# A fused attention and expert kernel: the second head's leftover keys moved to its front, and second scores of two row blocks formed on GpSimd

## The chip, the cores and the metric

The kernel runs on one core of a Trainium2 chip. The metric is device time in microseconds (us); a result is the median of several executions. Engines are called as in the profile: PE (TensorE matmul), PEld (its weight loads), DVE (VectorE), ACT (ScalarE), POOL (GpSimd) and SP (SyncE, which issues nearly all DMAs).

## The reference

Three layers, one behind the other:

```python
# attention, batch 4, heads 8, S = 576 tokens, head dimension 64
scores = scale * np.matmul(q, k.transpose(0, 1, 3, 2))
kth = np.partition(scores, -top_k, axis=-1)[..., -top_k:-top_k + 1]   # top_k = 32
scores = np.where(scores >= kth, scores, -1000000000.0)
attn = softmax(scores); x = np.matmul(attn, v)                        # -> (2304, 512)
# soft mixture of experts: 8 experts, 4 slots each
logits = x @ phi                                                      # 2304 x 32
d = softmax over tokens of logits; slot_input = d.T @ x
slot_out[e] = relu(slot_input[e] @ w1[e]) @ w2[e]
x = (softmax over slots of logits) @ slot_out
# a dense layer, 512 -> 2048 -> 512
h = x @ w_in; g = piecewise square of h; out = g @ w_out
```

Every row of scores keeps those of its 576 entries that reach the row's 32nd largest.

## The kernel before

**Tiling.** The 32 heads are worked on as 16 pairs. The two heads of a pair lie on partitions 0 to 63 and 64 to 127 of `qt` and `kt`. A head's 576 rows are four row blocks of 128 and 64 left over; the leftover rows of both heads form a fifth block (r = 4), so that a pair has nine tiles of 128x576 scores. The host lays out `kt` as 640 columns: 512 keys of both heads, then the last 64 keys of the first head, then the last 64 of the second, with zeros in the other head's half.

**Steps of a tile**, each a letter in a table of order; digits give block and head, as in `X31`.
- `S`, `C`: scores by matmul into `s_ps`, in two halves (`op_s`), copied by ACT to `ssb`.
- `G`, `L`: DVE takes the 8 largest of seven pieces of a row and, by maxima and replacements, the 24 largest of these (`top`).
- `M`: a mask `mb` of the entries that reach the 24th largest. Four tiles a pair have it on GpSimd (`MASK_POOL`), with ACT counting by a sum (`O`); the other five have mask and count on DVE.
- `X`: the **second scores** (`op_x`): the same scores once more into `x_ps`, and on top `nbig` times the mask, which pushes the masked entries far down. `Y`: DVE takes the 8 largest of what is left, ranks 25 to 32 (`op_y`, L406).
- `K`: a **rank pick** on 128x8 (`op_k`, L415): by the count it picks the 32nd largest. `B` (POOL) scales it, `P` (ACT) makes a penalty of what lies below, `U` (POOL, L429) subtracts it, `E` (ACT) is the exponential.
- `T`, `Q`: four transposes on PE and ACT's copy to `ptb`, for the product with `v` (`A`). In block 4 both heads' rows lie over the same 512 keys, so four transposes serve both. The leftover keys go through one more (`rem`, `R`).
- `l`: late steps of a finished pair (division, transposition into `xT`). `m`: steps of the expert work of a batch, after its fourth pair (`moe_acc`): logits with `phi` repeated four times to fill 128 columns (L568), running maximum, exponential, transposes and the product with x (L616).
- `c`: one piece of the 64-bit input weights is converted each frame, with one table addition on POOL (L220).

**Order.** `ORDER` is a table of such words; its last letter says by how many frames a step lags its pair's first. All words are run through once per frame, 16 pairs plus the lags, and PE, ACT, DVE and POOL each execute their instructions in just this order. PSUM is full: `s_ps`, `x_ps` and `pt_ps` have one buffer each, `m_ps` two banks.

**Weights.** 512 KB tiles of the experts' weights are loaded ahead into `NA` = 21 slots and some that come free towards the end of attention (`wfree`, `wload`); the rest follow when attention's memory is given up. If one of a row's pieces holds too many of the 32, or a like rare case, a flag sends the whole program through a slower version; the flag is not raised on these inputs.

```python
def op_x(u, j):                                  # cut
    if j == 0: both_heads(u, [(0, flat[0], 0), (1, flat[2], 0)]); ...
    nc.tensor.matmul(x[:, n]..., nbig, mb[:, c:c + NR * P], start=False, stop=True)
```

Of the kernel before, what the change touches and what calls it, by code (L numbers as in the profile page):

```python
# [8 lines left out]
F32 = mybir.dt.float32  # L9
# [28 lines left out]
QW = S + REM  # L38
NTILE = NPAIR * 9
# [10 lines left out]
NA = 21  # L50
# [4 lines left out]
MASK_POOL = ((0, 1), (1, 1), (2, 1), (4, 0))  # L55
# [3 lines left out]
M30c O21c S01b A30d E01c Q00c P10c Y21c T01c C01b G00b A31d P11c R0c L4c S10b M31c K20c me C10b  # L59
A40d Q01c G01b K21c c1b c3b H3d A41d H4d U10c U11c lDd M40c X30c X31c N2c Y30c c4b E10c E11c B2c  # L60
K30c me me N3c S11b Y31c T10c L0b A00c O40c C11b A01c Q10c P20c P21c lNd U20c K31c M00b T11c
S20b H0c B3c R1c Q11c C20b G10b E20c X40c lYd U21c P30c Y40c M01b lEd lXd S21b E21c lCd T20c z4b
X00b X01b Q20c G11b K40c C21b L1b U30c P31c T21c A10c Y00b E30c M10b Y01b S30b Q21c R2c O01b c5b
C30b G20b N4c B4c T30c U31c M11b P40c U40c E31c N1b K00b N0b A11c G21b S31b K01b L2b X10b Q30c
c2b B0b H1c X11b C31b T31c E40c Y10b M20b me c6b K10b P00b U00b P01b md S40b R3c md A20c Q31c
A21c me C40b M21b U01b O11b S00a md Y11b E00b H2c G30b T40c X20b G40b md c0a Q40c C00a G31b T00b
X21b K11b md R4c L3b B1b Y20b
# [6 lines left out]
def kernel_body(tc, qT, kT, vP, phi, w1, w2, w_in, w_out, out, fast, flag):  # L74
# [101 lines left out]
    cnt_all = p_moe.tile([P, NTILE], F32, name="cnt_all")  # L176
    kth_all = p_moe.tile([P, NTILE], F32, name="kth_all")

# [55 lines left out]
    def load_pair(pi):  # L234
        b, hp = divmod(pi, NHP)
        q, k = pair_in[pi] = [p_qkv.tile([P, QW], F32, name=t, tag=t) for t in ("qt", "kt")]
# [32 lines left out]
    def last_rows(u, o, c, z):  # L269
        q, k = q_of(u), pair_in[u[0]][1]  # L270
        n = min(z, NR * P) - c
        nc.tensor.matmul(o[:, :n], q, k[:, c:c + n], start=True, stop=True, skip_group_check=True)
        if z > NR * P:
            last_keys(u, o[:, n:])

    def last_keys(u, o):
        q, k = q_of(u), pair_in[u[0]][1]
        for jj in range(2):
            nc.tensor.matmul(o, q, k[:, NR * P + jj * REM:NR * P + (jj + 1) * REM], start=(jj == 0), stop=(jj == 1),
                             skip_group_check=True)  # L280
# [75 lines left out]
    def op_m(u, j):  # L356
# [6 lines left out]
        if (u[1], j) in MASK_POOL:  # L363
# [12 lines left out]
    def op_x(u, j):  # L376
        if not fast:
            return
        if j == 0:
            x = st[u]["x"] = ps_s.tile([P, 3, 8, REM], F32, name="x_ps", tag="x_ps", bufs=1)  # L380
            flat = [x[:, n].rearrange("p a b -> p (a b)") for n in range(3)]
            if u[1] == NR:
                last_rows(u, flat[0], 0, NR * P)
                last_keys(u, flat[1][:, :REM])
            else:
                both_heads(u, [(0, flat[0], 0), (1, flat[2], 0)])
# [33 lines left out]
    def op_b(u):  # L420
        kb = st[u]["kb"][:, :width[u[1]]]
        nc.gpsimd.tensor_scalar(kb, kb, BIG, None, op0=ALU.mult)  # L422
# [755 lines left out]
```

## Time and profile before

| | us |
|---|---|
| median of 3 runs (lowest, highest) | 869.44 (868.55, 871.07) |
| the profiled execution | 868.62 |
| its span, first to last instruction | 866.8 |
| of it PE busy | 823.2 |
| DVE, ACT, POOL busy | 674.8, 639.2, 422.8 |

The profiled execution is 0.8 us below the median, and 1.8 us of it lie outside the span. Busy shares are over the whole span, which has three stages with different loads: attention with the expert work of three batches (to about 550 us), the last batch and the experts' layers with their weight loads (to about 650), and the dense layer. PE's granted clock was 0.994 of full speed in the mean.

### The profile page before, as it was taken

The page shows a single profiled execution, that of the slowest core. Times are in us where ns is not written, and L with a number is a line of the kernel's source. Part 1 is how long each engine was busy: PE and PEld are TensorE (multiplying, and loading weights), DVE is VectorE, ACT ScalarE, POOL GpSimd, SP SyncE. Part 2 cuts the span into 40 slices and gives each one's busy share as a digit, 9 for nine tenths or more (in the row PEclk, how much of TensorE's full clock was granted, in tenths as well). Part 3 has the DMA queues.
Part 4 walks back from the last instruction along what each step waited for, and adds up shares of the span by engine and source line. Part 5 has one row for each costly group of instructions (what it writes and reads, how often), then busy time and mean ns, then how long its engine had stood idle before and what let it go on. Part 6 is the DMA issues. An engine that isn't in the chain of part 4 may idle for free.

```text
span 866.8 us, 16822 instructions
## 1 busy us (share of the span) xinstructions
PE 823.2 (95%) x5432; PEld 616.9 (71%) x5479; DVE 674.8 (78%) x3067; ACT 639.2 (74%) x1305; POOL 422.8 (49%) x448
## 2 busy tenths in 40 slices
PE   3799999999999999999999999889889999999996
PEld 2477777777777777777777787653257888888885
DVE  3899999997899998989998899525258886666663
ACT  2688898888888988888988989625249995545552
POOL 1587877785877876768776767301102210000000
PEclk9999999999999999999999999999999999999999
DMA  5223222222313313211211113559980001001011
GB/s 176 85 65 98 86 85 94 86 86 67 116 47 102 116 47 105 83 56 39 83 48 41 48 53 109 170 165 393 403 351 1 1 21 55 37 1 37 1 37 41
DMA packets 31155, 80.93 MB, mean 93 GB/s; under 512 B 5360, under 2 KB 5872, under 8 KB 31056
## 3 DMA queue, kind: packets, MB, share of 16 engines
q1 hardware_dynamic: 30768, 79.29, 26.9%
q8 instruction: 45, 0.74, 0.4%
q14 instruction: 54, 0.44, 0.2%
q10 hardware_dynamic: 288, 0.46, 0.2%
HBM read 70.60 MB, written 8.91 MB: 92 GB/s over the span
## 4 chain that ended last, share of the span: by engine, by line
PE 70%; POOL 8%; ACT 8%; DVE 7%; DMA 4%; issue 2%; SPq 1%; ACTq 0%; POOLq 0%; DVEq 0%
PE o_ps L991 21%; PE av_ps L476 12%; PE s_ps L266 9%; PE pt_ps L440 7%; POOL ssb L429 3%; PE x_ps L266 3%; PE x_ps L392 3%; POOL mb L364 2%; PE moe_ps L568 2%; PE av_ps L474 2%; PE h_ps L955 2%; PE h L824 2%; DMA w<-cv_d 2%; POOL tr L220 2%; DVE cand L306 2%
## 5 line engine op out<-in xcount | busy, mean ns | idle before, releaser
L991 PE MATMUL o_ps<-whl,ghl 128*128 128x512 f32 x864 | 217.3, 397 | 0.0
L429 POOL TENSOR_TENSOR ssb<-ssb,pen 128x576 f32<-128x576 f32 x141 | 179.8, 1280 | 76.2 <-ACT pen L426 73.3
L991 PEld LDWEIGHTS o_ps<-whl,ghl 128*128 128x128 f32 x864 | 161.8, 189 | 34.3 <-DVE ghl L975 0.3
L306 DVE MAX8 cand<-ssb 128x8 f32<-128x82 f32 (+1 forms) x1008 | 163.0, 227 | 14.6 <-ACT ssb L297 14.6
L476 PE MATMUL av_ps<-v_sb,ptb 128*128 128x65 f32 (+1 forms) x1280 | 141.6, 261 | 0.0
L476 PEld LDWEIGHTS av_ps<-v_sb,ptb 128*128 128x128 f32 (+1 forms) x1280 | 137.3, 181 | 0.0
L406 DVE MAX8 l<-x_ps 128x8 f32<-128x576 f32 x144 | 109.5, 760 | 32.6 <-PE x_ps L397 19.1
L266 PE MATMUL s_ps<-kt,qt 64*128 64x288 f32 (+2 forms) x768 | 112.1, 383 | 17.7 <-ACT ssb L297 13.2
L297 ACT COPY ssb<-s_ps 128x576 f32<-128x576 f32 x144 | 92.8, 644 | 42.0 <-PE s_ps L266 36.8
L364 POOL TENSOR_SCALAR mb<-ssb,top 128x576 bf16<-128x576 f32 x64 | 110.8, 1731 | 9.5 <-DVE top L313 9.5
L426 ACT ACTIVATE pen<-ssb,kb 128x576 bf16<-128x576 f32 x141 | 106.9, 787 | 2.5 <-POOL kb L422 2.5
L432 ACT ACTIVATE ssb<-ssb,nm 128x576 f32<-128x576 f32 x141 | 108.5, 784 | 0.0
L957 ACT ACTIVATE rg<-h_ps,half 128x384 f32<-128x384 f32 x96 | 55.6, 579 | 70.0 <-PE h_ps L955 67.1
L266 PEld LDWEIGHTS s_ps<-kt,qt 64*128 64x128 f32 x768 | 79.7, 192 | 37.6 <-ACT ssb L297 16.1
L454 ACT COPY ptb<-pt_ps 128x512 f32<-128x512 f32 x144 | 85.2, 591 | 11.7 <-PE pt_ps L440 11.6
L963 DVE SCALAR_TENSOR_TENSOR rg<-h_ps,rg 128x384 f32<-128x384 f32 x96 | 53.4, 556 | 50.0 <-ACT rg L958 50.0
L440 PE MATMUL pt_ps<-ident,ssb 128*128 128x128 f32 x576 | 90.1, 279 | 0.8
L942 POOL TENSOR_TENSOR tr_l<-tr_l 128x512 int32<-128x512 int32 x16 | 21.2, 1326 | 135.9 <-DVE tr_l L941 51.9
L266 PE MATMUL x_ps<-kt,qt 64*128 64x512 f32 x256 | 73.3, 640 | 2.1 <-DVE l L406 2.1
L440 PEld LDWEIGHTS pt_ps<-ident,ssb 128*128 128x128 f32 x576 | 64.1, 144 | 15.0 <-issue 7.2
L313 DVE MAX8 top<-cand 128x8 f32<-128x56 f32 x432 | 73.5, 206 | 0.1
L415 DVE SCALAR_TENSOR_TENSOR pick<-rank,cnt_all,l 128x8 f32<-128x8 f32 x144 | 66.6, 463 | 0.1
(172 smaller groups left out, 1263.8 us busy)
## 6 DMA issues: line engine op xcount, KB each, us to landing
w<-in_moe_w_dram SPq DMA_DIRECT2D x53, 512.0 KB, 6.7
x<-in_moe_w_in_dram SPq DMA_DIRECT2D x16, 512.0 KB, 3.9
w<-in_moe_w_out_dram SPq DMA_DIRECT2D x16, 512.0 KB, 10.2
w<-in_moe_w_dram SPq DMA_DIRECT2D x22, 256.0 KB, 6.2
v_sb<-in_v_dram SPq DMA_DIRECT2D x16, 325.0 KB, 3.0
kt<-in_k_dram SPq DMA_DIRECT2D x15, 320.0 KB, 2.9
qt<-in_q_dram SPq DMA_DIRECT2D x15, 320.0 KB, 3.3
out_dram<-o_sb SPq DMA_DIRECT2D x17, 256.0 KB, 2.2
```

The costliest lines, as they stand in the source:

```text
L266: nc.tensor.matmul(o, q[us], k[us, c:c + o.shape[-1]], start=True, stop=True, tile_position=(j * D, 0), skip_group_check=True)
L297: nc.scalar.copy(ssb[:, 0] if u[1] == NR else ssb[:, :, hf], st.pop((u, hf))[:, :, :HS])
L306: nc.vector.max(st[u]["cand"][:, j, 8 * g:8 * g + 8], row(u, j)[:, S * g // NSEG:S * (g + 1) // NSEG])
L364: nc.gpsimd.tensor_scalar(st[u]["mb"][:, j], row(u, j), t_u, None, op0=ALU.is_ge)
L406: nc.vector.max(st[u]["l8"][:, j], x[:, :S] if j == 0 else x[:, 3 * 512 - S:])
L426: nc.scalar.activation(pen, row(u, j), AF.Relu, bias=st[u]["kb"][:, j:j + 1], scale=-BIG)
L429: nc.gpsimd.tensor_tensor(row(u, j), row(u, j), st.pop((u, "pen", j)), op=ALU.subtract)
L432: nc.scalar.activation(row(u, j), row(u, j), AF.Exp, bias=st[u]["nm"][:, j:j + 1], scale=0.125)
L440: nc.tensor.transpose(pt[:, c, :], pr[:, c0:c0 + P], ident)
L454: nc.scalar.copy(ptb, st.pop((u, "pt", j)))
L476: nc.tensor.matmul(o, pj[:, c, sl], v_sb[:, 4 * jj + c, :], start=False, stop=(c == NR - 1), skip_group_check=True)
L991: nc.tensor.matmul(pos[t][n], a[:, sl], w, start=(f == 0 and k == 0), stop=(f == NF - 1 and k == 2))
```

## The change

1. **Leftover keys.** The second head's leftover keys are its first 64 instead of its last, and `kt` has 704 columns: the 576 keys of both heads in order, then the two leftovers block-diagonally. First scores need two matmuls of 288 columns a half in every block. The five-block layout stays, but block 4's two halves no longer share their 512 keys, so it has a second set of four transposes (`T41`) and two half copies (`Q40`, `Q41`).
2. **Second scores of blocks 3 and 4** (`BY_V`) are no longer made on PE. The mask is inverted (`is_lt`, always on DVE, with the count of lower entries), and GpSimd multiplies it with the scores into `w2` (new step `V`). `Y` reads `w2` from SBUF. This needs the 32nd largest to be positive; the flag now also tells of one that isn't.
3. **Expert logits** of batches 0 to 2 (`moe_quarters`): the four row blocks side by side in four column tiles of 32, so that logits and exponential work on 128x192 instead of 128x576; the maximum over the four quarters needs two more small transposes. The last batch keeps the old way.
4. **Order** and the rest: a new table (lags to `c`, `m` to `e`), other tiles for the masks on GpSimd, `NA` = 20.

```diff
-NA = 21
+NA = 20
-MASK_POOL = ((0, 1), (1, 1), (2, 1), (4, 0))
+MASK_POOL = ((0, 0), (0, 1), (1, 1), (2, 1))
+KW = S + P
+BY_V = (3, NR)
+NW2 = 2
 ORDER = '''
-M30c O21c S01b A30d E01c Q00c P10c Y21c T01c C01b G00b A31d P11c R0c L4c S10b M31c K20c me C10b
+O01b N4c md Y01b B4c T30c E31c N0b K00b M11b G21b c5b S31b Q30c X10b K01b B0b L2b X11b me c2b
...
 def op_s(u, hf):
-        if u[1] == NR:
-            for i in range(2):
-                last_rows(u, s[:, i, :HS], i * HS, (i + 1) * HS)
-        elif hf == 0:
-            both_heads(u, [(0, s[:, 0, :HS], 0), (1, s[:, 1, :REM], S), (1, s[:, 1, REM:HS], 0)])
-        else:
-            both_heads(u, [(0, s[:, 0, :n], HS), (1, s[:, 1, :HS], n), (0, s[:, 0, n:HS], NR * P)])
+        if u[1] < NR:
+            both_heads(u, [(j, s[:, j, :HS], hf * HS) for j in range(2)])
+            return
+        for i in range(2):
+            nc.tensor.matmul(s[:, i, :HS], q_of(u), pair_in[u[0]][1][:, i * HS:(i + 1) * HS], start=True, stop=True)
...
 def op_m(u, j):
+        if u[1] in BY_V:
+            nc.vector.tensor_scalar(st[u]["mb"][:, j], row(u, j), t_u, 0.0, op0=ALU.is_lt, op1=ALU.add,
+                                    accum_out=less_all[:, t:t + 1])
...
+    def op_v(u, j):
+        w = st[u, "w2", j] = p_hold.tile([P, S], F32, name="w2", tag="w2", bufs=NW2)
+        nc.gpsimd.tensor_tensor(w, row(u, j), st[u]["mb"][:, j], op=ALU.mult)
 def op_y(u, j):
+        if u[1] in BY_V:
+            src = st.pop((u, "w2", j))
...
 def op_t(u, j):
-        pr = row(u, j)
+        pr = row(u, j if r < NR else 0)
...
 def op_q(u, j):
+            sl = slice(j * REM, (j + 1) * REM)
+            nc.scalar.copy(st[u, "ptb", 0][:, :, sl], st.pop((u, "pt", j))[:, :, sl])
...
+    def moe_quarters(b):
+        for c in range(NHP):
+            for r in range(NR):
+                nc.tensor.matmul(ps[r * NSLOT:(r + 1) * NSLOT, :P], phi_sb[:, c, 0], xs[c][1][:, r * P:(r + 1) * P],
+                                 start=(c == 0), stop=(c == NHP - 1), tile_position=(0, r * NSLOT),
+                                 skip_group_check=True)
+        for c in range(NHP):
+            nc.tensor.matmul(ps[:NSLOT, P:], phi_sb[:, c, 0], xs[c][1][:, NR * P:], start=(c == 0), stop=(c == NHP - 1),
+                             tile_position=(0, 0), skip_group_check=True)
...
+        nc.scalar.copy(lq[:, :P], ps[:, :P])
+        nc.vector.reduce_max(mb, lq, axis=AX.X)
...
```

**PE, second scores of block 4.** In the frame before, PE makes the last block's second scores between first scores of the next pair and the late transposes (`x_ps` are second scores, `s_ps` first scores, `xT_ps` late transposes):

```order
L266 MATMUL s_ps<-kt,qt 128x224
L272 MATMUL x_ps<-kt,qt 128x512
L279 MATMUL x_ps<-kt,qt 128x64 x2
L392 LDWEIGHTS nbig
L392 MATMUL x_ps<-mb,nbig 128x512
L395 LDWEIGHTS nbig
L395 MATMUL x_ps<-mb,nbig 128x64
L229 MATMUL xT_ps<-ident,xh 64x64
```

With the change the late transposes stand among first scores, transposes of `ssb` and second scores of block 0 alone, and no second scores of blocks 3 and 4 are left:

```order
L274 MATMUL s_ps<-kt,qt 128x288 x2
L533 MATMUL xT_ps<-ident,xh 128x128 x4
L443 MATMUL pt_ps<-ident,ssb 128x128 x4
L449 MATMUL rem_ps<-ident,ssb 128x128
L274 MATMUL s_ps<-kt,qt 128x288 x2
L274 MATMUL x_ps<-kt,qt 128x512 x2
```

**POOL, the new products** (`w_...` is `w2`), in one frame of the change; three subtractions now stand in a row ahead of block 3's two products, and two ahead of block 4's:

```order
L432 TENSOR_TENSOR ssb<-ssb,pen 128x576 x3
L395 TENSOR_TENSOR w_3855<-ssb,mb 128x576
L346 TENSOR_SCALAR nm<-top 128x2
L395 TENSOR_TENSOR w_3873<-ssb,mb 128x576
L425 TENSOR_SCALAR kb<-kb 128x2
L224 TENSOR_SCALAR tr<-tr 128x512
L520 TENSOR_TENSOR xh<-xu,den 128x576
L432 TENSOR_TENSOR ssb<-ssb,pen 128x576 x2
L395 TENSOR_TENSOR w_3996<-ssb,mb 128x576
```

A frame on POOL has 15 two-input operations (`TENSOR_TENSOR`), of which three are the products; before it had 12.

**DVE, where it reads them**: block 3's two masks, a rank pick and two maxima over `x_ps`, then the first maximum over a product:

```order
L356 TENSOR_SCALAR mb,less_all<-ssb,top 128x576
L407 MAX l_1850<-x_ps 128x8
L356 TENSOR_SCALAR mb,less_all<-ssb,top 128x576
L418 SCALAR_TENSOR_TENSOR pick,kb<-rank_79,cnt_all,l_1850 128x8
L407 MAX l_1850<-x_ps 128x8
L407 MAX l_1883<-w_1871 128x8
```

The two masks release the two products; the third maximum waits for the first of them, and all that follows on DVE waits behind it.

## Rows read from the trace of the kernel before

**Rows 1.** The page: busy us, share of the span and instructions per engine.

```profile
PE 823.2 (95%) x5432; PEld 616.9 (71%) x5479; DVE 674.8 (78%) x3067; ACT 639.2 (74%) x1305; POOL 422.8 (49%) x448
```

**Rows 2.** The chain in order of time: start us, us, what.

```profile
318.70 1.23 POOL tr L220
...
389.43 1.23 POOL tr L220
...
413.05 0.74 PE s_ps L266 x5
...
421.81 1.23 POOL tr L220
...
577.08 12.04 PE h L824 x96
```

**Rows 3.** Busy times by stretch; the first row names the columns.

```profile
core 0: us, PE busy (x) PEld busy (x) DVE busy (x) ACT busy (x) POOL busy (x), PEclk, DMA share, GB/s
389.43:421.81 32.38, 32.22 (x241) 24.69 (x246) 30.43 (x169) 28.82 (x60) 25.41 (x28) 1.00 0.18 57
318.70:389.43 70.73, 70.42 (x551) 54.12 (x559) 62.67 (x339) 60.11 (x127) 50.82 (x56) 1.00 0.24 75
525.00:577.00 52.00, 45.89 (x385) 36.70 (x386) 32.78 (x153) 36.39 (x92) 20.74 (x24) 1.00 0.42 128
577.00:648.00 71.00, 63.43 (x385) 25.57 (x386) 27.74 (x60) 26.10 (x53) 5.71 (x4) 0.95 0.99 384
```

**Rows 4.** PE's timeline in one frame: start us, us, engine, line, operation, count.

```profile
395.69 1.13 PE L266 MATMUL x_ps<-kt,qt 64*128 64x512 f32 x4
396.74 0.49 PE L388 MATMUL x_ps<-kt,qt 128*128 128x128 f32 x2
...
397.56 0.61 PE L440 MATMUL pt_ps<-ident,ssb 128*128 128x128 f32 x4
398.00 0.27 PE L446 MATMUL rem_ps<-ident,ssb 128*128 128x128 f32 x1
398.11 1.03 PE L272 MATMUL s_ps<-kt,qt 128*128 128x288 f32 x4
...
399.37 0.44 PE L474 MATMUL av_ps<-v_sb,rs 128*128 128x130 f32 x2
...
409.08 0.87 PE L266 MATMUL s_ps<-kt,qt 64*128 64x288 f32 x6
409.88 0.33 PE L472 MATMUL av_ps<-v_sb,rs 128*64 128x65 f32 x2
...
417.62 1.13 PE L272 MATMUL x_ps<-kt,qt 128*128 128x512 f32 x2
...
419.31 0.24 PE L229 MATMUL xT_ps<-ident,xh 64*64 64x64 f32 x1
```

**Rows 5.** Timelines of DVE and of POOL in the same frame.

```profile
394.45 0.21 DVE L415 SCALAR_TENSOR_TENSOR pick<-rank,cnt_all,l 128x8 f32<-128x8 f32 x1
395.61 0.91 DVE L415 SCALAR_TENSOR_TENSOR pick<-rank,cnt_all,l 128x8 f32<-128x8 f32 x1
410.34 0.22 DVE L415 SCALAR_TENSOR_TENSOR pick<-rank,cnt_all,l 128x8 f32<-128x8 f32 x1
...
395.22 1.28 POOL L429 TENSOR_TENSOR ssb<-ssb,pen 128x576 f32<-128x576 f32 x1 [0.95 <-ACT pen L426]
409.59 1.73 POOL L364 TENSOR_SCALAR mb<-ssb,top 128x576 bf16<-128x576 f32 x1 [0.20 <-DVE top L313]
```

**Rows 6.** The rank pick by its source line (ns min/median/max), and two groups of the page.

```profile
L415 DVE SCALAR_TENSOR_TENSOR pick<-rank,cnt_all,l x144: 199/221/1199, 30.7 to 553.3; 128x8 f32<-128x8 f32 x144
...
L415 DVE SCALAR_TENSOR_TENSOR pick<-rank,cnt_all,l 128x8 f32<-128x8 f32 x144 | 66.6, 463 | 0.1
...
L454 ACT COPY ptb<-pt_ps 128x512 f32<-128x512 f32 x144 | 85.2, 591 | 11.7 <-PE pt_ps L440 11.6
```

**Rows 7.** DVE's timeline in the last batch's expert work.

```profile
563.71 0.42 DVE L580 TENSOR_REDUCE mb<-lT 128x1 f32<-128x256 f32 x1
```

More of the change, by code (lines that the diff above doesn't have):

```diff
@@ L235, in load_pair @@
         b, hp = divmod(pi, NHP)
-        q, k = pair_in[pi] = [p_qkv.tile([P, QW], F32, name=t, tag=t) for t in ("qt", "kt")]
+        q, k = pair_in[pi] = [p_qkv.tile([P, w], F32, name=t, tag=t) for t, w in (("qt", QW), ("kt", KW))]
         if pi == 0:
@@ new lines, in weigh @@
+    def weigh(pu, xs, et, main, mid):
+        parts = [(et[:, r, :], slice(2 * r, 2 * r + 2), slice(0, P)) for r in main]
+        if mid:
+            parts += [(er[:, jj, :], slice(8, 9), slice(jj * D, (jj + 1) * D)) for jj in range(2)]
+        for n, (w, rs, cs) in enumerate(parts):
+            for hp in range(NHP):
+                nc.tensor.matmul(pu[hp * NSLOT:(hp + 1) * NSLOT, cs], w,
+                                 xs[hp][0][:, rs, :].rearrange("p a d -> p (a d)"), start=(n == 0 or not main),
+                                 stop=(n >= len(main) - 1), tile_position=(0, hp * NSLOT), skip_group_check=True)
@@ L547, in bank, with join_quarters, moe_last @@
+    def join_quarters():
+        ps = ps_m.tile([P, P], F32, name="rq_ps", tag="m_ps")
+        nc.tensor.matmul(ps[:, :1], same.rearrange("p r s -> p (r s)"), run_q, start=True, stop=True)
+        nc.vector.tensor_copy(run_s, ps[:, :1])
+    def moe_last(b, pieces, pool):
         def bank():
-            if pool is None:
-                return ps_m.tile([P, 512], F32, name="moe_ps", tag="m_ps")
             nbank[0] += 1
@@ L553, in moe_acc @@
         xs = [x_of[b * NHP + hp] for hp in range(NHP)]
-        first = nrun[0] is None
         c0, c1 = pieces[0][0], pieces[-1][1]
@@ L588, in moe_acc @@
         nc.scalar.activation(eT[:, c0:c1], lT[:, c0:c1], AF.Exp, bias=nm, scale=1.0, accum_out=sb)
-        if not first:
-            al = p_moe.tile([P, 1], F32, name="al", tag="al", bufs=3)
-            nc.scalar.activation(al, before, AF.Exp, bias=nm, scale=-1.0)
+        al = p_moe.tile([P, 1], F32, name="al", tag="al", bufs=3)
+        nc.scalar.activation(al, before, AF.Exp, bias=nm, scale=-1.0)
         yield
@@ L610, in moe_acc @@
         pu = bank()[:, :P]
[L611 to L625 removed]
+        weigh(pu, xs, et, main, mid)
+        yield
+        nc.vector.scalar_tensor_tensor(acc, acc, al, pu, op0=ALU.mult, op1=ALU.add)
+        nc.vector.scalar_tensor_tensor(run_s, run_s, al, sb, op0=ALU.mult, op1=ALU.add)
         yield
@@ L671, in emit @@
             calls[k]((pi, int(name[1])), *([int(name[2])] if len(name) > 2 else []))
-            if k == "X" and pi >= NPAIR - 2:
+            if k in "SX" and pi >= NPAIR - 2:
                 nx[pi] = nx.get(pi, 0) + 1
-                if nx[pi] == 9:
-                    wfree.append(qk_slot)
-                    wload(1)
+                if nx[pi] == 9 + 2 * sum(r not in BY_V for r in range(NR)):
+                    wfree.extend([qk_slot] + [ssb_slot] * (NSSB - 5) * (pi == NPAIR - 1))
+                    wload(99)
             if pi == NPAIR - 1:
@@ L718, in kernel_body @@
     wload(99)
-    share = {}
-    gens = [moe_acc(B - 1, [(lo, hi)], ps_s, share) for lo, hi in ((0, 2 * P), (2 * P, NR * P), (NR * P, S))]
+    join_quarters()
+    gens = [moe_last(B - 1, [(lo, hi)], ps_s) for lo, hi in ((0, 2 * P), (2 * P, NR * P), (NR * P, S))]
     run(gens[0])
```

245 lines of the change are left out of this document (140 added, 105 removed).

## The prediction

> **What bounds the kernel now.** I read the page first: over the span PE is busy 95%, DVE 78%, ACT 74%, POOL 49% [rows 1]. That is a mean over stages, so I then took the busy times by stretch. The attention part repeats one frame per head pair. From one table addition of the conversion to the next (the chain passes it in every frame) it takes 421.81 - 389.43 = 32.38 us [rows 2], and in that stretch PE is busy 32.22 us, DVE 30.43, ACT 28.82, POOL 25.41 [rows 3]. PE has 0.16 us to spare, DVE 1.95. So TensorE sets the frame, and VectorE stands 6% below it: what the change can win a frame is read from the second row, not from the first. Two frames, one of which also carries the expert work of a batch, take 389.43 - 318.70 = 70.73 us, 5.97 more than two plain ones [rows 2]; DVE is busy only 62.67 us of them, PE 70.42 [rows 3]. So the expert work is paid at PE's price.
>
> The first expert product starts at 577.08 [rows 2]. Less three times 5.97 us that is 17.27 frames of 32.38 us. Behind it come 71 us in which the DMA engines are 99% busy at 384 GB/s [rows 3], and then the dense part, which the change leaves alone.
>
> **PE, per frame.** Each price is the distance between two starts of one frame's timeline [rows 4].
> - The second scores of row block 3 go: 397.56 - 395.69 = 1.87 us. Those of block 4 go: 419.31 - 417.62 = 1.69 us.
> - The eight first-score steps of blocks 0 to 3 lose two matmuls each. One kind takes 409.88 - 409.08 = 0.80 us, the other 0.74 [rows 2]. What two matmuls side by side cost without a third is seen at 512 columns: 396.74 - 395.69 = 1.05 us, so 288 columns come to 0.59. Gain 4 x 0.21 + 4 x 0.15 = 1.44 us.
> - Block 4's first scores go from 640 columns to 576: 1.26 us (399.37 - 398.11) times 64/640 is 0.13 us.
> - Four more transposes for block 4 cost 398.00 - 397.56 = 0.44 us.
>
> Sum: 4.69 us less, PE 32.22 - 4.69 = 27.5 us a frame. PE stops being the bound, and the next question is which engine is.
>
> **POOL, per frame.** Three products of 128x576 are new. The nearest row, the subtraction of the same shape, takes 1.28 us [rows 5]: 25.41 + 3 x 1.28 = 29.25 us. Four masks a frame stay on GpSimd, as before, on other tiles. **ACT**: block 4's copy of its transposes, 0.591 us [rows 6], becomes two copies of half the columns; between nothing more and one whole copy more, I take 0.15, as a half copy is nearer a half than a whole: 29.0 us. Neither passes DVE.
>
> **DVE, per frame.** It keeps nine maxima over 576, five masks and nine rank picks; three maxima now read the product in SBUF instead of PSUM, which I cost at nothing either way. But DVE's 30.43 us hold waiting that the view counts as busy. The rank pick works on 8 columns, yet its 144 executions last 199 ns at least and 463 ns in the mean [rows 6]. In the timeline [rows 5], the pick at 394.45 meets no GpSimd product and takes 0.21 us; the one at 395.61 starts inside the subtraction of 395.22 and ends at 396.52, just behind the subtraction's end at 396.50. So a pick waits for a running two-input operation of GpSimd. Nine picks wait 9 x 0.26 = 2.4 us a frame, and DVE's own work is 28.0 us.
>
> GpSimd now issues 15 two-input operations a frame instead of 12, in a frame that is a little shorter. At random phase the wait grows by 15/12 x 32.38/31.3 = 1.29, to 0.34 us a pick or 3.1 us a frame. The lower bound is 2.4 (the new order keeps the picks as clear as before), the upper 0.7 a pick (each waits as long as the one at 395.61), 6.3 us. I take 3.1, since before the waits lay as a random phase makes them. To 28.0 + 3.1 I add 0.2 us of idle waits, between 0 and today's 1.95: a binding engine is rarely idle (PE: 0.16 now). **The new frame is 31.3 us, bound by DVE.**
>
> The Trainium skill ("SBUF — State Buffer", the rules on the shared port pair) says that a VectorE instruction with two SBUF inputs and any GpSimd instruction that reads SBUF exclude each other for the whole instruction. The trace bears this out for two-input operations only: the pick at 410.34 starts inside the one-input mask of 409.59 to 411.32 and takes 0.22 us [rows 5]. By the page the masks would block as well, GpSimd would be in the way 29 of 31 us, and the sum would be that of the slow rival below; by the rows it is 31.3 us.
>
> **Where the new work stands.** The order on DVE has block 3's two masks, then a rank pick and two maxima, and then the first maximum over a GpSimd product; on POOL that product stands behind three subtractions in a row, which wait for ACT. If POOL runs late there, DVE stands, and with it all the maxima behind. POOL has 31.3 - 29.25 = 2 us to catch up in a frame, where it had 7. That is the weak place of the new frame.
>
> **Expert work.** The logits of three batches go from two products of 128x288 by four to 16 matmuls of 32x128, four side by side, and four of 32x64. PE, with 3.8 us to spare, should hide them and what follows. DVE gets five small operations instead of four, the widest a maximum over 192 columns (0.42 us at 256 [rows 7]); ACT gets some more copies. I take 2.3 us a batch instead of 5.97, between 0 and 5.97: nearer the lower end, as only what the binding engine does counts. Gain 3 x 3.7 = 11.0 us.
>
> **Edges.** By the places in the table of order a pair's way from its first score to its last output takes 2.20 frames instead of 2.29; up to 0.09 x 31 = 2.8 us, I take half, 1.4. One weight slot of 0.52 MB fewer is loaded ahead, so 0.52 MB more have to pass in the stage where DMA is saturated: at 384 GB/s 1.4 us more [rows 3]. Keys grow by 10%; their queue has room in attention (DMA share 0.18), so nothing.
>
> **Sum.** 17.27 frames x (32.38 - 31.3) = 18.7 us, plus 11.0, plus 1.4, less 1.4: 29.7 us less. The profiled execution took 868.62 us, so 838.9; the median of the runs stands 0.8 above it: **839.7 us.**
>
> **Rivals.**
> - *Picks stay clear* (0.14): no pick meets a new product, waits stay under 2.4 us and the frame falls to 30.2, one us above POOL's work. For it: the picks' phase is fixed by the order, and 410.34 shows clear ones. Against: 29 us of POOL leave little gap. 17.27 x 2.18 + 11.0 + 2.8 - 1.4 = 50 us less, 819.
> - *POOL and DVE hold each other up* (0.22): the products come late behind the subtractions and DVE is idle for another 0.7 us; frame 32.0. For it: POOL is the fullest it has been, and its subtractions wait for ACT today. 17.27 x 0.38 + 11.0 - 1.4 = 16 us less, 853.
> - *Nothing left* (0.05): waits eat the whole frame's gain (32.38) and most of the expert gain, 3 to 4 us remain for the lost slot and a longer tail; 868.
> - *Slower* (0.09): the pick at nearly every start runs into a GpSimd operation, as at 395.61, nine times 0.7 us. DVE needs 28.0 + 6.3 = 34.3 us a frame: 17.27 x 1.92 = 33.2 more, 11.0 less, 1.4 more: 893. It decides from a frame of 33.0 us on, that is picks of 0.73 us in the mean instead of 0.46. Against it: 12 products in 32.38 us gave 0.46.
> - The forecast (0.50): frames of 30.7 to 31.9, so 829 to 850.
>
> **How the numbers follow.** A difference under 0.3%, 2.6 us, can't be told from none. Faster: 0.50 + 0.14 + 0.22 = 0.86; the same 0.05; slower 0.09. The range takes the forecast, half of the better rival and nearly all of the third: 820 to 858.
>
> **What would show it.** Right: PE busy near 27.5 of a frame of 31.3 us, DVE over 98%, POOL near 29; picks near 0.54 us in the mean; a frame with expert work at most 2.5 us longer than one without; 71 us of saturated DMA as before. Wrong: DVE idle before the maxima over the products by more than 1 us a frame (the third rival), picks above 0.73 us (the slower one), PE still over 99% busy (then the matmuls removed were not what its time went to), or picks at 0.4 us with a frame near 30.

## The result and the profile after

| | before | after |
|---|---|---|
| median of the runs shown with the result, us | 869.36 (868.55 to 871.07, 4 runs) | 821.39 (818.45 to 827.39, 4 runs) |
| ratio of after to before, 95% interval | | 0.9455 (0.9398 to 0.9511) |
| profiled execution: time, span, us | 868.62, 866.8 | 827.39, 825.6 |
| a plain frame, us | 32.38 | 30.06 |
| expert work of a batch, us | 5.97 | 1.44 |
| first expert product, us | 577.08 | 537.63 |
| from there to the end of the span, us | 289.7 | 288.0 |

The kernel is 48 us faster, 18 us more than forecast; 821.4 lies in the range (820 to 858), near its lower end. The profiled execution of after is the slowest of its four, 6 us above their median. I work out terms on it, and read nothing from a difference under 6 us between the whole times of two single executions; behind the first two frames its plain ones repeat within 0.05 us.

From the page of after: the engines' busy lines (they answer to [rows 1]), the granted clock in 40 slices, and the chain by engine and line.

```profile
PE 767.6 (93%) x5022; PEld 556.4 (67%) x5022; DVE 670.0 (81%) x3084; ACT 634.5 (77%) x1328; POOL 482.6 (58%) x496
...
PEclk9879999999999999999999996789999999999999
...
DVE 50%; PE 43%; ACT 3%; issue 2%; DMA 2%; SPq 1%; POOL 0%; ACTq 0%; POOLq 0%; DVEq 0%
```

The chain now runs over DVE for half of the span, although DVE is busy only 81% of it: again a mean over stages. Next, POOL's timeline of after, the table addition that marks a frame (start us, us, engine, line, operation, names, shapes); it answers to the marks of [rows 2].

```profile
22.13 1.26 POOL L228 TENSOR_TENSOR tr<-tr 128x512 int32<-128x512 int32 x1
56.65 1.27 POOL L228 TENSOR_TENSOR tr<-tr 128x512 int32<-128x512 int32 x1
...
117.25 1.28 POOL L228 TENSOR_TENSOR tr<-tr 128x512 int32<-128x512 int32 x1
147.31 1.27 POOL L228 TENSOR_TENSOR tr<-tr 128x512 int32<-128x512 int32 x1
177.36 1.27 POOL L228 TENSOR_TENSOR tr<-tr 128x512 int32<-128x512 int32 x1
...
238.92 1.28 POOL L228 TENSOR_TENSOR tr<-tr 128x512 int32<-128x512 int32 x1
...
482.57 1.27 POOL L228 TENSOR_TENSOR tr<-tr 128x512 int32<-128x512 int32 x1
```

Frames of 30.06 and 30.05 us stand one behind the other. Two frames with a batch's expert work between them take 238.92 - 177.36 = 61.56 us, 1.44 more than two plain ones. The first frame takes 34.52 us.

The busy times by stretch of after (columns as in [rows 3]): a plain frame, the two frames with expert work, the end of attention, a piece of that end, and the 71 us with saturated DMA.

```profile
117.25:147.31 30.06, 28.09 (x213) 20.52 (x209) 30.02 (x167) 28.63 (x62) 29.14 (x32) 1.00 0.31 96
177.36:238.92 61.56, 58.78 (x476) 42.79 (x472) 61.46 (x338) 58.34 (x130) 58.27 (x61) 1.00 0.30 96
482.57:537.63 55.06, 47.47 (x330) 38.62 (x326) 27.54 (x128) 30.81 (x81) 19.23 (x22) 0.76 0.38 130
500.00:508.00 8.00, 6.93 (x32) 6.18 (x32) 1.51 (x9) 4.79 (x11) 3.98 (x5) 0.50 0.34 128
538.00:609.00 71.00, 64.61 (x393) 26.71 (x385) 29.93 (x63) 28.01 (x55) 6.17 (x5) 0.95 0.97 384
```

In the plain frame DVE is busy 30.02 of 30.06 us; PE has 2 us to spare, where DVE had them before. POOL shows 29.14. That looks like room of 0.9 us, but POOL's timeline of the frame goes from one operation to the next, with one wait of 0.15 us; the rest is gaps under 0.15 us around small operations. Four operations in a row show such gaps, 0.08 and 0.09 us:

```profile
138.09 1.92 POOL L359 TENSOR_SCALAR mb<-ssb,top 128x576 bf16<-128x576 f32 x1
140.09 0.22 POOL L425 TENSOR_SCALAR kb<-kth_all 128x2 f32<-128x2 f32 x1
140.40 1.73 POOL L359 TENSOR_SCALAR mb<-ssb,top 128x576 bf16<-128x576 f32 x1
142.10 0.23 POOL L346 TENSOR_SCALAR nm<-top 128x2 f32<-128x2 f32 x1
```

So two engines are full at once; that POOL by itself needs all of the frame is tested below.

The groups of after's DVE and POOL, each a line with its shapes (busy us, mean ns of one, idle before); the picks answer to [rows 6].

```profile
L407 DVE MAX8 l<-x_ps 128x8 f32<-128x576 f32 x96 | 72.1, 751 | 4.7 <-PE x_ps L389 4.5
L418 DVE SCALAR_TENSOR_TENSOR pick<-rank,cnt_all,l 128x8 f32<-128x8 f32 x96 | 40.1, 418 | 0.0
L407 DVE MAX8 l<-w 128x8 f32<-128x576 f32 x48 | 35.4, 738 | 0.0
L418 DVE SCALAR_TENSOR_TENSOR pick<-rank,less_all,l 128x8 f32<-128x8 f32 x48 | 25.4, 530 | 0.0
...
L432 POOL TENSOR_TENSOR ssb<-ssb,pen 128x576 f32<-128x576 f32 x141 | 178.6, 1285 | 3.8 <-ACT pen L429 2.6
L395 POOL TENSOR_TENSOR w<-ssb,mb 128x576 f32<-128x576 f32 x48 | 61.7, 1285 | 1.1 <-DVE top L305 0.9
```

The new products take 1.285 us, the same as the subtractions of their shape. The maxima that read them cost 738 ns against 751 from PSUM, and none waits for its product. The 144 picks take 65.5 us, 455 ns in the mean, where before they took 463: **their waits did not grow**, although GpSimd has a quarter more two-input operations.

Two picks of the plain frame, and what POOL did beside them (timelines of after, DVE then POOL):

```profile
129.01 0.92 DVE L418 SCALAR_TENSOR_TENSOR pick<-rank,cnt_all,l 128x8 f32<-128x8 f32 x1
139.36 0.20 DVE L418 SCALAR_TENSOR_TENSOR pick<-rank,less_all,l 128x8 f32<-128x8 f32 x1
...
128.62 1.28 POOL L395 TENSOR_TENSOR w<-ssb,mb 128x576 f32<-128x576 f32 x1
138.09 1.92 POOL L359 TENSOR_SCALAR mb<-ssb,top 128x576 bf16<-128x576 f32 x1
```

The first starts inside a product and ends at 129.93, just behind the product's end at 129.90. The second starts 1.27 us after the start of a one-input mask and takes 0.20. Over the whole execution 57 of the 144 picks take more than 0.3 us: each of them starts inside a two-input operation of POOL and ends 0.01 to 0.03 us behind its end.

### The profile page after: what moved, and what is told of

The parts are those of the page before. It is cut to its first block, busy times and chain, and to the rows that moved or that the text cites. A ratio compares the mean times of both kernels' runs of the same rounds, so it can differ in the third digit from the quotient of the medians.

```text
span 825.6 us, 16081 instructions
## 1 busy us (share of the span) xinstructions
PE 767.6 (93%) x5022; PEld 556.4 (67%) x5022; DVE 670.0 (81%) x3084; ACT 634.5 (77%) x1328; POOL 482.6 (58%) x496
## 3 DMA queue, kind: packets, MB, share of 16 engines
q1 hardware_dynamic: 31344, 79.81, 27.8%
## 4 chain that ended last, share of the span: by engine, by line
DVE 50%; PE 43%; ACT 3%; issue 2%; DMA 2%; SPq 1%; POOL 0%; ACTq 0%; POOLq 0%; DVEq 0%
PE o_ps L1065 24%; DVE cand L298 15%; DVE l L407 9%; DVE pick L418 6%; DVE cand L303 5%; DVE top L305 5%; DVE mb L356 3%; PE av_ps L484 3%; DVE mb L361 2%; PE h_ps L1029 2%; PE h L898 2%; PE pt_ps L443 2%; PE s_ps L274 2%; PE so L921 1%; PE x_ps L274 1%
## 5 line engine op out<-in xcount | busy, mean ns | idle before, releaser
L484 PE MATMUL av_ps<-v_sb,ptb 128*128 128x65 f32 (+1 forms) x1280 | 147.0, 266 | 0.0
L484 PEld LDWEIGHTS av_ps<-v_sb,ptb 128*128 128x128 f32 (+1 forms) x1280 | 142.2, 187 | 1.8
L274 PE MATMUL s_ps<-kt,qt 64*128 64x288 f32 x512 | 102.2, 478 | 17.1 <-ACT ssb L289 12.7
L443 PE MATMUL pt_ps<-ident,ssb 128*128 128x128 f32 x640 | 103.2, 285 | 10.2 <-ACT ptb L459 8.6
L443 PEld LDWEIGHTS pt_ps<-ident,ssb 128*128 128x128 f32 x640 | 72.8, 148 | 38.3 <-ACT ptb L459 13.2
L459 ACT COPY ptb<-pt_ps 128x512 f32<-128x512 f32 x128 | 75.1, 587 | 3.8 <-PE pt_ps L443 3.7
L407 DVE MAX8 l<-x_ps 128x8 f32<-128x576 f32 x96 | 72.1, 751 | 4.7 <-PE x_ps L389 4.5
L274 PEld LDWEIGHTS s_ps<-kt,qt 64*128 64x128 f32 x512 | 41.0, 195 | 42.6 <-ACT ssb L289 23.0
L395 POOL TENSOR_TENSOR w<-ssb,mb 128x576 f32<-128x576 f32 x48 | 61.7, 1285 | 1.1 <-DVE top L305 0.9
L1049 DVE TENSOR_TENSOR ghl<-rg,ghl 128x384 fp32r<-128x384 f32 x96 | 55.3, 576 | 6.0
```

The source lines that it names most:

```text
L274: nc.tensor.matmul(o, q[us], k[us, c:c + o.shape[-1]], start=True, stop=True, tile_position=(j * D, 0), skip_group_check=True)
L407: nc.vector.max(st[u]["l8"][:, j], src)
L443: nc.tensor.transpose(pt[:, c, :], pr[:, c0:c0 + P], ident)
L484: nc.tensor.matmul(o, pj[:, c, sl], v_sb[:, 4 * jj + c, :], start=False, stop=(c == NR - 1), skip_group_check=True)
```

## The experiments

Nine picks of 0.455 us hold 9 x 0.255 = 2.3 us of waiting over a clear pick's 0.20 (a mean over all frames; in the plain frame shown it is 2.5), so DVE's own work in a frame is 30.06 - 2.3 = 27.8 us. The questions: which of the two full engines sets 30.06, are the picks' waits really the lock read from [rows 5], what did each part of the change bring, and what was lost at the two ends of attention. Ratios are to the kernel before on the same chip, with medians from 868.1 to 869.4 us. For frames I give the distance of the marks, as above (without the conversion on POOL, that of DVE's shifts).

### Relief for POOL, for DVE, for both

**No negated maxima on POOL.** Five small operations go.

```diff
-        nc.gpsimd.tensor_scalar(nm[:, :n], st[u]["top"][:, :n, 0], -0.125, None, op0=ALU.mult)
+        st[u]["nm"] = zero2
```

> The changed kernel without the five small operations a frame (128x2 and 128x1) in which GpSimd makes the negated row maximum; the exponential has a bias of zero instead. Each held POOL for 0.2 to 0.3 us with the gap behind it, so POOL's frame falls from 30.0 us, gaps counted, to 28.6 to 28.9; DVE, PE and ACT keep their work. Theory A (POOL paces the frame, and DVE's own full 30 us are in part the picks' waiting for POOL): the frame falls to 28.8 to 29.6, the time by 6 to 18 us. Theory B (DVE and POOL are both full at 30.0 us, each by itself): the frame stays at 29.9 to 30.1 and the time at 819 to 823.

818.99 us (818.14 to 821.37), ratio 0.9437 (0.9419 to 0.9455); the frame is 30.43 us, longer than 30.06. **No last pick of block 4** (its maximum over the product and its pick left out, the product kept):

```diff
 def op_y(u, j):
+        if u[1] == NR:
+            st.pop((u, "w2", j))
+            return
 def op_k(u, j):
+        if fast and u[1] == NR:
+            return
```

> The changed kernel without the maximum over block 4's product and without its rank pick; its threshold stays at a constant 1, so its rows keep other entries. DVE has 0.66 us for the maximum and 0.2 to 0.9 for the pick less in a frame, POOL, ACT and PE the same. Theory (DVE binds, POOL stands right behind it with 29.1 us): the frame falls from 30.06 to 29.2 to 29.4 and the time by 11 to 15 us, to 806 to 811. Rival (POOL, or DVE and POOL in turn, bind): the frame stays at 29.8 or more, the time at 817 or more.

813.49 us (812.28 to 814.16), 0.9364 (0.9348 to 0.938); frame 30.00 us. The frame is the rival's, the time lies between the two forecasts. The 8 us that are gone all the same are not in the plain frames: in its profile a batch costs 0.1 us instead of 1.44, and from the last mark to the first expert product it is 46.8 us against 55.1 in after's profiled execution, its longest. What shortened that end was not tested. **Both:**

> Both reliefs at once: no negated row maxima on POOL, and neither the maximum over block 4's product nor its pick on DVE (its threshold stays a constant 1). Theory A: the frame is that of the run without row maxima or up to 0.3 us less. Theory B (each of two full engines holds the frame alone, so that only both reliefs move it): the frame falls to 28.8 to 29.3, though each relief alone left it at 30.0; time 798 to 806.

823.11 us (821.18 to 827.39), 0.9483 (0.945 to 0.9516); frame 30.45 us. **The conversion's three operations on POOL left out:**

```diff
-                nc.gpsimd.tensor_scalar(tf, tf, 2.0 ** -15, None, op0=ALU.max)
+                pass
...
-                nc.gpsimd.tensor_tensor(t, t, r, op=ALU.add)
...
-                nc.gpsimd.tensor_tensor(tf, tf, sg, op=ALU.mult)
+                pass
```

> The changed kernel without the three operations a frame (1.49, 1.27 and 1.16 us) with which GpSimd converts a piece of the input weights; DVE's shift stays. POOL's frame falls from 30.0 to about 26; 13 two-input operations are left instead of 15. Under both theories DVE sets the frame then: its own 27.6 us plus the picks' waits. If the waits follow how much of a frame two-input operations fill, they are 2.5 x 13/15 = 2.2 and the frame is 29.7 to 29.9; if POOL's being full itself stretched DVE's frame, it falls to 28 to 29.4. Time 800 to 818.

809.56 us (807.54 to 811.71), 0.9332 (0.9309 to 0.9355); frame 29.47 us.

Busy times over about two plain frames (columns as in [rows 3]), first without the negated maxima:

```profile
87.00:147.00 60.00, 55.59 (x410) 40.52 (x414) 59.93 (x328) 55.82 (x119) 55.50 (x49) 1.00 0.30 97
```

Then without the last pick of block 4:

```profile
87.00:147.00 60.00, 56.11 (x417) 41.28 (x420) 58.21 (x327) 56.88 (x121) 58.29 (x61) 1.00 0.30 96
```

Without the conversion on POOL:

```profile
87.00:147.00 60.00, 56.69 (x426) 42.11 (x429) 59.53 (x343) 57.88 (x123) 51.79 (x55) 1.00 0.28 97
```

Without the pick DVE has room (58.21 of 60), and the frame stays at 30.00: **POOL alone needs 30.0 us.** Without the negated maxima POOL has room (55.50), yet DVE is full and the frame longer. The picks say why. Group lines of DVE, without the negated maxima:

```profile
L419 DVE SCALAR_TENSOR_TENSOR pick<-rank,cnt_all,l 128x8 f32<-128x8 f32 x96 | 46.5, 484 | 0.0
L419 DVE SCALAR_TENSOR_TENSOR pick<-rank,less_all,l 128x8 f32<-128x8 f32 x48 | 23.3, 485 | 0.0
```

With both reliefs:

```profile
L424 DVE SCALAR_TENSOR_TENSOR pick<-rank,cnt_all,l 128x8 f32<-128x8 f32 x96 | 68.7, 715 | 0.1
L424 DVE SCALAR_TENSOR_TENSOR pick<-rank,less_all,l 128x8 f32<-128x8 f32 x32 | 12.1, 379 | 0.0
```

The frame less its waits over 0.20 us a pick: after 30.06 - 2.30 = 27.8; without the negated maxima 30.43 - 9 x 0.284 = 27.9; without the conversion (picks of 382 ns in the mean) 29.47 - 1.64 = 27.8; with both reliefs, one pick and one maximum fewer, 30.45 - 8 x 0.431 = 27.0. So DVE's own work is constant within 0.1 us in the first three, and the waits came back in the place of what was saved. My expectations held only in part. The negated maxima were to shorten the frame or leave it at 30.0, and it got longer; the time, 818.99, is not to be told from the change's. Both reliefs together were to bring 28.8 to 29.3 or leave the frame as it was without the maxima, and it stayed there (30.45 against 30.43). Without the conversion the frame did fall, by 0.59 us, between the two forecasts (28 to 29.4 and 29.7 to 29.9), as the picks' waits fell to 1.64 us; the time lies in the forecast span. So relief for POOL helped where the picks happened to become clear, and not where they met other operations. The waits hang on where the picks fall, more than on how many operations POOL has.

Not only on products, either. With both reliefs a pick in each plain frame stands right behind the start of a one-input mask (DVE, then POOL):

```profile
83.30 0.70 DVE L424 SCALAR_TENSOR_TENSOR pick<-rank,cnt_all,l 128x8 f32<-128x8 f32 x1
...
83.24 1.74 POOL L360 TENSOR_SCALAR mb<-ssb,top 128x576 bf16<-128x576 f32 x1
```

It takes 0.70 us and ends at 84.00, 0.76 us after the mask's start and 0.98 us ahead of its end. The kernel before has the same thing, which I had overlooked:

```profile
34.88 0.70 DVE L415 SCALAR_TENSOR_TENSOR pick<-rank,cnt_all,l 128x8 f32<-128x8 f32 x1
...
34.82 1.73 POOL L364 TENSOR_SCALAR mb<-ssb,top 128x576 bf16<-128x576 f32 x1
```

In all runs, picks with both tensors in SBUF that start 0.04 to 0.5 us after a mask's start end 0.75 to 0.77 us after it, and the 395 that start 0.6 to 1.6 us after it take 0.23 us at most. A mask too holds a pick up, in its first 0.76 us.

### The lock itself

The pick gets one tensor from SBUF instead of two (it becomes another instruction of the same size), and the negated maxima stay out of POOL.

```diff
-            nc.vector.scalar_tensor_tensor(st[u]["pick"][:, j], rank8[:, int(v)], (cnt_all, less_all)[v][:, t:t + 1],
-                                           st[u]["l8"][:, j], op0=ALU.is_equal, op1=ALU.mult, accum_out=kth)
+            nc.vector.tensor_scalar(st[u]["pick"][:, j], st[u]["l8"][:, j], (cnt_all, less_all)[v][:, t:t + 1], None,
+                                    op0=ALU.min, op1=ALU.max, accum_out=kth)
```

> The changed kernel, with two parts left out: GpSimd's negated row maxima (the exponential's bias is zero), as in the run that left out these alone, and the choice by rank in the pick, which becomes an operation of the same size with ONE tensor input from SBUF (the least of the product's eight values and the count, largest of the eight). GpSimd keeps its two-input operations, where they stood. Theory A (a pick waits only because both of its tensors come from SBUF while GpSimd runs an operation with two such tensors; what was saved on GpSimd alone came back as longer picks): all nine picks of a frame stay at about 0.2 us, VectorE needs its own 27.7 us, GpSimd 30.0 less 5 x 0.3 = 28.5, ScalarE 28.5, so the frame is 28.6 to 29.2 us against 30.43 without the negated maxima alone: 17.3 frames less by 1.2 to 1.8 us, 788 to 799 us. Theory B (the picks' length is not a lock between the two engines but a fixed cost or a wait for something else, and VectorE's stream takes 30.4 us whatever the pick reads): frame 30.4 us, 815 to 823 us. Theory C (the pick gets short, and another engine holds the frame at 30): 812 us and more, with VectorE's busy share under 96%.

798.58 us (796.62 to 799.3), 0.9184 (0.9164 to 0.9203): theory A, at the upper end of its time. The frame is 28.98 us, 1.45 less than the same kernel with two-input picks. The pick's line of DVE (ns min/median/max, first and last start):

```profile
L419 DVE TENSOR_SCALAR_CACHE_REDUCE pick<-l,cnt_all x96: 198/205/223, 25.5 to 475.3; 128x8 f32<-128x8 f32 x96
...
L419 DVE TENSOR_SCALAR_CACHE_REDUCE pick<-l,less_all x48: 190/202/221, 42.4 to 482.4; 128x8 f32<-128x8 f32 x48
```

Not one of 144 takes over 0.223 us, where after's longest take over a microsecond, though 94 of them start inside a two-input operation of POOL. With the lock away and the same relief for POOL, which alone had lengthened the frame, it is 1.08 us shorter than the change's. POOL now sets it: in the frame from 82.57 to 111.55 POOL has no gap over 0.10 us, and DVE is busy 28.42 of 28.98. One-input picks without the relief were not run.

### The parts of the change

**Block 3's second scores back on PE.**

```diff
-BY_V = (3, NR)
+BY_V = (NR,)
...
-... V30b ... V31b ...
+... X30b ... X31b ...
```

> The changed kernel with block 3's second scores back on PE (words X30 and X31, and Y30 behind them); block 4's stay on GpSimd. PE's frame rises by 1.87 us from 28.1 to 30.0, POOL's falls by 2 x 1.28 to 26.6, DVE's stays at 30.0. Theory (the gain came from taking work off PE until DVE bound): PE and DVE are level, so the frame lies between 30.1 and 31.0 and the time between 822 and 838. Rival (PE's load no longer matters at all): frame 30.06, 821. Rival (the load on GpSimd holds the new frame): the frame falls below 30, 815 or less.

824.02 us (820.44 to 824.84), 0.9473 (0.9448 to 0.9498); frame 30.41 us, PE busy 58.47 of 60 us, DVE 57.79, POOL 52.79. Frame and time lie in the theory's spans; the time alone is not to be told from the change's (818.45 to 827.39), the frame is. PE is the fullest engine again, at 97%. Of the frame's 2.32 us, block 3's products bring 0.35 and all the rest 1.97: their place on PE costs 1.87 us, but what they free runs against POOL and DVE at once. How the 1.97 divides among block 4's products, the leftover keys and the order was not tested.

**The old logits of 128 columns in the new order.** The diff puts the old generator back for the three batches.

> The changed kernel with the expert logits of batches 0 to 2 made the old way (128 columns wide, 576 tokens), in the new order. Theory (a batch now costs 1.5 us instead of 6.0 since PE has 2 us a frame to spare and needs little): PE gets about 4 us a batch more, more than the 2 us it has to spare, so a batch costs 3 to 6 us and the time is 5 to 13 us longer, 826 to 834. Rival (DVE binds, and PE's part hides either way): within 2 us of 821.

838.11 us (835.8 to 838.69), 0.9636 (0.9617 to 0.9656); plain frames of 30.02 us, and a batch costs some 8 us. That is more than I expected (3 to 6 us a batch, 826 to 834 us). The column tiles and their order are worth 16.7 us, more than the 11.0 of the forecast. The words' places were made for the new form, so the old one may stand worse here than it would in an order of its own.

### The ends of attention

TensorE's granted clock, 1.00 in a plain frame, stands at 0.50 from 500 to 508 us of after, and at 0.53 from 36 to 50. Idle products of 256 columns ahead of scores and transposes were to hold it, for the first and last pair, then for the last alone.

```diff
+WARM = (0, NPAIR - 1)        # second run: (NPAIR - 1,)
...
+            nc.tensor.matmul(o[:, :WCOL], ident, w, start=True, stop=True, skip_group_check=True)
```

> The changed kernel with one idle product on PE (128 by 256 columns, float32, overwritten by the real one) ahead of every first-score half, second-score step and set of transposes of the first and the last pair. Theory (the frames are bound by DVE, and the change gave some of its gain back at both ends, where PE ran at half its granted clock from 36 to 50 us and again between 498 and 541 us): the granted clock stays at 1.00 at both ends, its mean rises from 0.969 to 0.99 or more, the frame stays 30.06 us, and the time falls from 821.4 to 811 to 817. Rival (the ends are set by waits for ACT, DVE and DMA, whatever PE's clock): the clock rises, but the time stays at 820 to 825, or grows by the 0.5 us that each of some 40 idle products takes.

> The changed kernel with idle products on PE (128 by 256 columns) ahead of the last pair's scores and transposes only. With them in both ends the last 55 us of attention took 52 and the first stretch 4 us more. Theory (at the end PE's clock costs more than the idle products): the granted clock of 498 to 541 us rises to 0.95 or more and the time falls to 816 to 820. Rival (the idle products cost what the clock gives): 820 to 825.

831.49 us (828.81 to 832.52), 0.9571 (0.9557 to 0.9586), and 822.65 (821.13 to 824.76), 0.9481 (0.9461 to 0.9501). The stretches 36 to 50 and 498 to 541 us of the second run:

```profile
36.00:50.00 14.00, 11.51 (x81) 8.12 (x82) 14.00 (x75) 11.80 (x23) 12.54 (x12) 1.00 0.04 16
498.00:541.00 43.00, 36.61 (x299) 25.27 (x299) 12.14 (x46) 18.76 (x55) 4.62 (x6) 0.92 0.52 174
```

The clock came back (in the second run at the start too, where nothing was added), and no time with it. In the first run the added products themselves hold up the start: its first frame takes 35.85 us. So the first theory failed, and for the last pair alone the rival holds: the lower clock at the ends is real, but giving it back this way brings nothing that can be told from the change's own spread. From 36 to 50 us DVE is busy for all of the 14.00 us at either clock, so there PE's clock did not set the pace; what it costs at the end of attention stays open.

### A version that keeps the computation

**Eight largest in PSUM.** For blocks 0 to 2 they go into unused columns of the product's own PSUM tile, so that the pick has one tensor from SBUF; three of five negated maxima go to DVE.

```diff
-            st[u]["l8"] = p_small.tile([P, 2, 8], F32, name="l8", tag="l8")
+            st[u]["l8"] = (p_small.tile([P, 2, 8], F32, name="l8", tag="l8") if u[1] in BY_V else
+                           st[u]["x"][:, 1, P:P + 16].rearrange("p (j k) -> p j k", k=8))
...
+NM_DVE = (0, 2, 4)
+        eng = nc.vector if u[1] in NM_DVE else nc.gpsimd
```

> The changed kernel, computing all of it: for row blocks 0, 1 and 2, whose second scores come from TensorE, the eight largest are written into the unused columns of the same PSUM tile, so that their picks have one tensor from SBUF and one from PSUM; and the negated row maxima of blocks 0, 2 and 4 are taken on VectorE instead of GpSimd. Theory A (lock between two-input operations, both engines full): the six picks of blocks 0 to 2 take 0.2 us each, the three others 0.2 to 0.9; VectorE needs 27.7 + 3 x 0.3 + 3 x 0.16 = 29.1 us a frame, GpSimd 30.0 less 3 x 0.3 = 29.1, so the frame is 29.1 to 29.5 us: 804 to 812 us against 821. Theory B (no lock, or the PSUM operand does not avoid it): the six picks keep a mean over 0.35 us, frame 30.0 to 30.5 us, 819 to 828 us. Theory C (the tile in PSUM now comes free only after its pick, and TensorE's next product waits for it): picks 0.2 us, but VectorE idle over 0.3 us a frame, frame 29.8 us and more, 816 us and more.

848.53 us (847.13 to 850.93), 0.9769 (0.975 to 0.9789). The picks' lines of DVE (ns min/median/max):

```profile
L421 DVE SCALAR_TENSOR_TENSOR pick<-rank,cnt_all,x_ps x96: 198/210/225, 24.7 to 524.7; 128x8 f32<-128x8 f32 x96
...
L421 DVE SCALAR_TENSOR_TENSOR pick<-rank,less_all,l x48: 200/365/1029, 42.9 to 531.1; 128x8 f32<-128x8 f32 x48
```

One kernel, one instruction, one size: with an operand in PSUM the longest takes 0.225 us, with both in SBUF 1.029. The operand in PSUM is clear in the same place, too: 31 of those 96 start inside a two-input operation of POOL. That is the lock, shown a second time. But PE's waits of the same run have

```profile
PE x_ps L275 <- DVE pick L421: 30.7, 17, 2.1
```

(us in total, times, longest): the tile comes free only with a late pick, theory C. **Three picks moved forward** in the order of work (`K01b` here; `K11b` goes behind `Y11b`, `K21b` behind `Y21b` in the same way):

```diff
-N0b K00b M11b G21b c5b S31b Q30c X10b K01b B0b
+N0b K00b K01b M11b G21b c5b S31b Q30c X10b B0b
```

> The run before it (the eight largest of blocks 0 to 2 in the unused columns of their PSUM tile, three row maxima negated on VectorE), with three picks moved: the second picks of blocks 0, 1 and 2 stand on VectorE right behind the first pick, or behind their own search for the eight largest, where the second pick of block 0 stood 1.2 us later, that of block 1 behind seven searches of a segment, that of block 2 behind a search of the other kind. So the PSUM tile comes free some 0.2 us after the last search. All of the computation is done. Theory A (two-input lock, both engines full; the run before lost only because TensorE's next product waited for a late pick, 38.5 us of such waits): VectorE's idle time for the product falls from 40 us to under 10, the six picks stay at 0.2 us, VectorE needs 29.1 us a frame and GpSimd 29.1, frame 29.1 to 29.6 us, 804 to 814 us against 821. Theory C (holding the tile for the picks at all costs the frame): frame over 29.9 us, 819 us and more.

820.83 us (818.59 to 828.24), 0.947 (0.9436 to 0.9504). DVE's idle time before those maxima falls from 40.7 to 7.3 us, the six picks stay at 0.22, the plain frame is 29.65: 0.05 over theory A's bound, and the time misses it by 7 us. Other frames lost what this one won: two of the three batches cost 3.1 us each instead of 1.44, and one frame without expert work takes 31.26. The negated maxima on DVE took 0.13 to 0.47 us each (0.26 in the mean, not the 0.35 that the next expectation takes). **Those three on ScalarE:**

> The run before it, with the three row maxima of blocks 0, 2 and 4 negated on ScalarE instead of VectorE, where each had taken 0.35 us. All of the computation is done. Theory A (the engine that is fullest sets the frame, and the picks of blocks 0 to 2 no longer wait): VectorE gives up 1.05 us a frame, ScalarE takes 3 x 0.22 more on its 28.2, GpSimd stays at 29.1 with its gaps: frame 29.2 to 29.5 us instead of 29.65, so 3 to 8 us less, 812 to 818 us. Theory C (what is taken off one engine comes back as a wait of another, TensorE's product and the three remaining picks among them): frame 29.65 us or more, 819 us and more.

816.69 us (811.47 to 820.56), 0.94 (0.937 to 0.9429); frame 29.57, between the two theories, the time in theory A's span. By the medians it is 5 us below the change, but the intervals overlap: that it beats the change is not shown.

## Why the prediction was right, and where not

- **PE is relieved and DVE takes over: right.** PE went from 32.22 to 28.09 us a frame (27.5 forecast), DVE from 30.43 of 32.38 to 30.02 of 30.06. That POOL would be full beside it was not forecast.
- **The new products: right.** 1.285 us each, nothing extra for the maxima over them, and no wait before them. The weak place I named did not break.
- **The term that was off: "At random phase the wait grows by 15/12 x 32.38/31.3", 3.1 us a frame.** It measured 2.3. The phase is not random: the order repeats in every frame, and so does the place of each pick against POOL. In the plain frame four of nine picks wait 0.4 us or more, and the others run clear. The frame came out as in the rival "picks stay clear" (30.06, there 30.2), to which I gave 0.14, and by my own signs, picks of 0.455 us with a frame of 30.06 stand between "right" (0.54) and "wrong" (0.4 with a frame near 30). With waits of 2.3 the same sum, 28.0 + 2.3, gives 30.3. Over the 15 frames from 22.13 to 482.57 that is 15 x 1.24 = 19 us less than forecast.
- **Luck in the total.** With the measured frame and batch the sum is 17.27 x 2.32 + 3 x 4.53 = 53.7 us less, 815.7, outside the range of 820 to 858. The measured 821.4 is inside it because the ends came out some 6 us worse than forecast. One error paid for part of the other.
- **"For two-input operations only": wrong.** I read that from one pick, at 410.34, which starts 0.75 us into its mask. In the same trace the pick at 34.88 starts 0.06 us into one and takes 0.70. The sum scaled the waits by two-input operations alone.
- **POOL's load was read too low.** I took 29.25 us of busy time for room of 2 us. Without a pick the frame stays at 30.00 with POOL back to back. So POOL's floor stood at 30.0 us, and by this, waits that vanished altogether would have brought the frame 0.06 us, not 2.3 (an inference from that run; no run takes the lock away alone).
- **Expert work: 1.44 us a batch instead of the 2.3 taken**, 2.6 us over three batches; of the right kind, and the old form in the new order shows what it is worth.
- **Edges: no gain seen.** I had 1.4 us of gain from a shorter pass, and the 17.27 frames let all the time up to the first expert product shrink like plain frames: they are (577.08 - 3 x 5.97) / 32.38. From the last mark to the first expert product it is 52.2 us before (524.86 to 577.08) and 55.1 after; the first frame took 1.0 us more than a plain one before (33.41) and takes 4.5 now. Together some 6 us given back in the profiled execution, which itself lies 6 us above the median; with idle products for the last pair, and plain frames of 30.02, the same two stretches were 52.1 and 32.8. So how much the median execution loses there isn't shown. The clock is lower there, but the runs that restored it gained nothing; the cause stays open.
- **The saturated transfers: as before, without the 1.4 us more.** 0.97 of the DMA engines are busy for 71 us (0.99 before), and from there to the end it is 288.0 us against 289.7; a lost slot's 1.4 us can't be seen in one execution.

The Trainium skill ("SBUF — State Buffer", "Who interferes with whom") says that a VectorE instruction with two SBUF inputs contends with a GpSimd instruction that reads SBUF, and one with at most one such input, outside the two-port modes, does not. The runs agree on VectorE's side (0.225 us against 1.029); on GpSimd's side a two-input operation holds the pick to its end, and a one-input mask does so for its first 0.76 of 1.73 us: the mask of 83.24 with both reliefs held a pick for 0.5 us, the one at 138.09 let a pick that came later through in 0.20.

## What to carry to other kernels

When relief moves the bound to two engines that lock each other out, count the waits inside "busy" apart (duration less the shortest one of its kind), and expect them to come back when one engine alone is relieved; take the lock away, by putting one operand elsewhere, before counting on the gain. That worked here with parts of the work left out; with all of it kept, no gain is shown. An engine at 94 to 97% busy may be full: walk its timeline for waits instead of subtracting. In an order that repeats, contention has a fixed phase; average formulas bound it, they don't place it.

## What the hardware showed that I had not expected

- The plain shift on DVE (`tensor_scalar`, one input, 128x512) waits for POOL too, although it has one input. It takes 0.407 us at least. In the change it takes about 0.57: the one at 137.84 starts inside the product of 136.83 and ends 0.28 us behind the product's end, and the mask that POOL starts meanwhile takes 1.92 instead of 1.73. With one-input picks it started early in a product that ended at 102.93, and it took 1.06, again to 0.29 us behind that end. Whether it runs in one of the two-port modes that the rule above sets apart, no run shows. From DVE's timelines of the change and of that run:

```profile
137.84 0.57 DVE L226 TENSOR_SCALAR tr<-tr 128x512 int32<-128x512 int32 x1
...
102.16 1.06 DVE L228 TENSOR_SCALAR tr<-tr 128x512 int32<-128x512 int32 x1
```

  The masks on DVE, `tensor_scalar` with an accumulator, take 0.79 to 0.81 us in every run, whatever POOL does.
- In the profiled execution of the change TensorE's granted clock was at half at both ends of attention (0.53 from 36 to 50 us, 0.66 from 498 to 541); before, it was 1.00 from 36 to 50 and at the end of attention, from 525 to 577.
- With the change, four executions spread by 9 us (818.45 to 827.39), before by 2.5; on other chips the kernel before spread by up to 5. With idle products for the last pair the spread is 3.6 us, at mean clocks of 0.983 to 0.992. The executions with a lower mean clock tend to be the longer ones: the change took 827.39 us at 0.969 and 818.45 at 0.981, and the last run's six took 811.47 to 814.54 at 0.979 to 0.989, 818.83 to 820.56 at 0.975 and 0.976. That the clock makes the spread was not tested apart.
